# Two heads' states as one block-diagonal operand, diagonal blocks on GpSimd, and a later place for the weights' check

## The chip, the cores and the metric

The kernel runs on one core of a Trainium2 chip. The metric is the time of one execution on the device, in microseconds (us), as the median of several runs.

## The reference, cut to what matters

Three stages follow each other: a linear recurrence per head (four batches, eight heads, 768 steps, head width 48), a gated feed-forward block with a convolution along the sequence, and a sparse attention over four experts. The change touches the first stage alone.

```python
state = np.zeros((B, H, D, D), dtype=np.float32)
for t in range(S):
    kt, vt, rt, wt = (k[:, :, t], v[:, :, t], r[:, :, t], w[:, :, t])
    cur = np.einsum('bhd,bhe->bhde', u[None] * kt, vt)
    y[:, :, t] = np.einsum('bhd,bhde->bhe', rt, state + cur)
    state = wt[:, :, :, None] * state + np.einsum('bhd,bhe->bhde', kt, vt)
...
h = np.maximum(x @ w_in, 0.0)
...
gate = 1.0 / (1.0 + np.exp(-conv_out))
return (h * gate @ w_out).astype(np.float32)
```

## The kernel before, in words

Phase 1 does the recurrence and the feed-forward block together, and then the attention runs by itself. The recurrence is cut into 32 units. A unit is one pair of heads (`hp`, four of them), one half of the sequence (`h`) and one batch; units 0 to 3 are the first half of batch 0, units 4 to 7 its second half, and so on. A unit holds three chunks of 128 steps. Two heads of width 48 lie on the 128 partitions, head j = 0 on partitions 0 to 63 and head j = 1 on 64 to 127.

The program is written as 32 slots and a few more for what is left over; `slot(u)` fixes the order of all instructions on PE, DVE, ACT and POOL by hand. Each of these engines runs its list in that order. In slot u stand the second part of unit u, the first part of unit u + 1 and, from slot 5, two groups of the feed-forward block (`ga` and `ga + 1`, with `ga = 2u - 11`). For a unit the steps are:

- `scan_d`, `scan_f`, `queries` (one slot earlier, DVE, L230 to L245): running products of the decays, and from them K and Q.
- `bonus` (POOL, L250 and L251) and `diag` (DVE, L259), for units from 10 on: the diagonal entry e of each step, one number per head, chunk and step. Units below 10 get e from a product on PE (L302, moved to SBUF by ACT, L304).
- `blocks` (ACT, L266, six instructions a unit): writes e on the diagonal of AT, a 128 x 128 block per head and chunk.
- `scores` (PE, L282) and `masked` (DVE, L288): the entries below the diagonal go into AT.
- `trans`, `state` (PE, L297 and L315): U, the contribution of each chunk to the state. `carry1` (ACT, L322) scales it and moves it from PSUM to `Ss`, with three instructions for a unit with h = 0 and two for one with h = 1. `carry2` (DVE, L329) runs the recurrence over the chunks.
- `yout` (one slot later, PE): L343 multiplies AT with the values; L349 multiplies the state before a chunk with Q, for each head by itself:

```python
for j in range(2 if c else 0):
    p = slice(64 * j, 64 * j + 64)
    nc.tensor.matmul(y[p, cc], Sb[p, c - 1], t["Q"][p, cc], start=False, stop=(cc == CH - 1), ...)
```

- `rows`: Y is moved out of PSUM by ACT (L361), its rest is formed by DVE (L362), and POOL copies four edge columns: before the rest, for h = 1 (L359), or after it, for h = 0 (L365).
- `check` (ACT, L273): bounds on the decays.

In a feed-forward group PE multiplies (L387, nine rows a group), ACT takes the relu and the first tap (L391, L395), DVE adds the other two taps (L406 and L408, or L410 and L411), ACT takes the tanh (L414), DVE multiplies (L424), and PE multiplies again four groups later (L437, six rows). The product hs of L387 has one PSUM buffer.

The raw weights are loaded twice: for the conversion in slots 1 to 9 (`WS`, DVE L82, L83 and L197, POOL L84), and once more for `check_w` (ACT, L208 and L209 over 128 x 768 numbers), which stands in the slots of `WC2`, after the tanh of group ga and the gate and before `carry1`. The load is issued one slot earlier. In a slot with a check the order on ACT is thus tanh of ga, L208, L209, L322, L361, and DVE's L362 needs what L361 writes.

Below, the "mark" of a slot is the start of DVE's L362 in it. The mark of slot u belongs to unit u - 1.

Of the kernel before, what the change touches and what calls it, by code (L numbers as in the profile page):

```python
# [10 lines left out]
F32 = mybir.dt.float32  # L11
# [4 lines left out]
AF = mybir.ActivationFunctionType  # L16
OP = mybir.AluOpType
# [3 lines left out]
B, H, S, D = 4, 8, 768, 48  # L21
DM, FF = 384, 1024
NE, HD = 4, 64
C = 128
NC = S // C
# [4 lines left out]
CH = NC // 2  # L30
# [8 lines left out]
LAG = 4  # L39


X2_ON_DVE, V_ON_DVE, OUT_ON_DVE = (), (1,), (5,)
SCALED_ON_POOL = 13
BONUS_ON_PE = 10


def _f(ap):
# [47 lines left out]
def phase1(tc, nc, a, x2, ident, stat, lim, top, right, left2):  # L95

    s1 = ExitStack()
    cst = s1.enter_context(tc.tile_pool(name="cst", bufs=1, side="left"))
# [12 lines left out]
    T = {}  # L111
    fl = lambda ap: ap.rearrange("p a b -> p (a b)")

    def split(u):
        return u // (2 * HP), u // HP % 2, u % HP

    def load(u):
# [8 lines left out]
        z = ld.tile([128, NRKV], F32, name="rkv")  # L126
        zn = 2 * CH * 64 if u < BONUS_ON_PE else NRKV
        nc.sync.dma_start(z[:, 0:zn], a["rkv"][q, h][:, 0:zn])
# [11 lines left out]
    for j in range(2):  # L140
# [14 lines left out]
                            channel_multiplier=-1)  # L155
    msk = cst.tile([128, CH, C], U32, name="msk")
    nc.vector.tensor_copy(msk, ones3)
    Ss = []
    for i in range(HP):
        t = cst.tile([128, NC - 1, 64], F32, name=f"Ss{i}")  # L160
        nc.gpsimd.memset(t, 0.0)
        Ss.append(t)
    load(1)
# [6 lines left out]
    win = [wt.tile([128, 4, 3, 256], F32R, name=f"win{i}") for i in range(2)]  # L170
    wout = wt.tile([128, NF, DM], F32, name="wout")
    wl = lambda t: t.rearrange("p a b c -> p (a b c)") if len(t.shape) == 4 else t.rearrange("p a b -> p (a b)")

    def load_w(n, i):
        t = RW[n, i] = raw.tile([128, WC], U64 if wide else F32, name="rawt")
        nc.sync.dma_start(t, a[n][i])
# [50 lines left out]
    def scan_d(u):  # L227
        t = T[u]
        t["Dp"] = wk.tile([128, CH, C + 1], F32, name="Dp")
        nc.vector.tensor_tensor_scan(fl(t["Dp"]), t["w"][:, 0:NW], fl(cD), 0.0, op0=OP.mult, op1=OP.add)  # L230
# [16 lines left out]
    def bonus(u):  # L247
        b, h, hp = split(u)
        m = T[u]["rn"]
        nc.gpsimd.tensor_tensor(m, m, T[u]["kn"], op=OP.mult)  # L250
        nc.gpsimd.tensor_tensor(m, m, u_b[:, hp][:, :, None].to_broadcast([128, 2, CH, D]), op=OP.mult)  # L251

    def diag(u):
        t = T[u]
        if u < BONUS_ON_PE:
            nc.vector.tensor_tensor(t["k"], t["k"], t["r"], op=OP.mult)
            return
        e = t["e"] = wk.tile([128, 2, CH], F32, name="e")
        nc.vector.tensor_reduce(e, t["rn"], axis=AX.X, op=OP.add)  # L259

    def blocks(u):
        t = T[u]
        AT = t["AT"] = wk.tile([128, 2, CH, C], F32, name="AT")
        for j in range(2):
            for c in range(CH):
                nc.scalar.activation(AT[:, j, c], ident, AF.Copy, scale=t["e"][:, j, c:c + 1])  # L266

    def check(u):
        t = T[u]
        w, Fp = t["w"], t["Fp"]  # L270
        wc = w[:, 1:].rearrange("p (c t) -> p c t", c=CH)[:, :, 0:C]
        for z in range(2):
            nc.scalar.activation(Fp[:, :, 0:C], wc, AF.Relu, bias=lim[:, z:z + 1], scale=(-1.0, 1.0)[z],  # L273
                                 accum_out=stat[:, 2 * u + z:2 * u + z + 1])
# [15 lines left out]
    def trans(u):  # L290
        b, h, hp = split(u)
        t = T[u]
        n = CH - h
        m = ps_m.tile([128, CH * 128 + 2 * CH], F32, name="m")
        kt = m[:, 0:CH * 128].rearrange("p (c t) -> p c t", c=CH)
        for c in range(n):
            nc.tensor.transpose(kt[:, c], t["K"][:, c], ident)  # L297
        KT = t["KT"] = wk.tile([128, CH, 128], F32, name="KT")
        if u < BONUS_ON_PE:
            es = m[:, CH * 128:].rearrange("p (j c) -> p j c", j=2)  # L300
            for c in range(CH):
                nc.tensor.matmul(es[:, :, c], t["k"][:, c], u_c[:, hp], start=True, stop=True)  # L302
            e = t["e"] = wk.tile([128, 2, CH], F32, name="e")
            nc.scalar.activation(e, es, AF.Copy)  # L304
        nc.scalar.activation(KT[:, 0:n], kt[:, 0:n], AF.Copy)
# [12 lines left out]
    def carry1(u):  # L318
        b, h, hp = split(u)
        t = T[u]  # L320
        for c in range(CH - h):
            nc.scalar.activation(Ss[hp][:, CH * h + c, 0:D], t["U"][:, c], AF.Copy, scale=t["Dp"][:, c, C:C + 1])  # L322

    def carry2(u):
        b, h, hp = split(u)
        Sb = Ss[hp]
        for c in range(CH * h, CH * h + CH - h):
            if c:
                nc.vector.scalar_tensor_tensor(Sb[:, c, 0:D], Sb[:, c - 1, 0:D], T[u]["Dp"][:, c - CH * h, C:C + 1],  # L329
                                               Sb[:, c, 0:D], op0=OP.mult, op1=OP.add)  # L330

    YP = {}

    def yout(u):
        b, h, hp = split(u)
        t = T[u]
        y = ps_m.tile([128, CH, C], F32, name="m")
        Sb = Ss[hp]

        for cc in range(CH):  # L340
            for j in range(2):
                p = slice(64 * j, 64 * j + 64)
                nc.tensor.matmul(y[p, cc], t["v"][:, cc, j], t["AT"][:, j, cc], start=(cc == 0), stop=False,  # L343
                                 skip_group_check=True)
        for cc in range(CH):
            c = CH * h + cc
            for j in range(2 if c else 0):
                p = slice(64 * j, 64 * j + 64)
                nc.tensor.matmul(y[p, cc], Sb[p, c - 1], t["Q"][p, cc], start=False, stop=(cc == CH - 1),  # L349
                                 skip_group_check=True)  # L350
        t["y"] = y

    def rows(u):
# [44 lines left out]
    def conv(g):  # L398
        if not 0 <= g < NG:
            return  # L400
        bh, f = divmod(g, NF)
        h = bh % 2
        (ht, ct), w = G[g], cw[0]
        o, N = 2 * h, HT - 2 + 4 * h
        if h == 0:
            nc.vector.scalar_tensor_tensor(ct[:, 1:N], ht[:, 0:N - 1], w[:, 0, f:f + 1], ct[:, 1:N],  # L406
                                           op0=OP.mult, op1=OP.add)
            nc.vector.scalar_tensor_tensor(ct, ht[:, 1:N + 1], w[:, 2, f:f + 1], ct, op0=OP.mult, op1=OP.add)  # L408
        else:
            nc.vector.scalar_tensor_tensor(ct, ht[:, 1:N + 1], w[:, 0, f:f + 1], ct, op0=OP.mult, op1=OP.add)  # L410
            nc.vector.scalar_tensor_tensor(ct[:, 0:N - 1], ht[:, 3:N + 2], w[:, 2, f:f + 1], ct[:, 0:N - 1],  # L411
                                           op0=OP.mult, op1=OP.add)
        st = ml.tile([128, HT + 2], F32, name="st", bufs=2)[:, 0:N]
        nc.scalar.activation(st, ct, AF.Tanh)  # L414
        G[g] = ht, st
# [13 lines left out]
    def mlp2(g):  # L429
# [9 lines left out]
        if f == NF - 1:  # L439
# [13 lines left out]

    WS = ((1, "win", 0), (2, "win", 1), (3, "win", 2), (4, "wout", 0), (5, "win", 3), (6, "wout", 1), (7, "wout", 2),
          (8, "wout", 3))
    WC2 = tuple((10 + i, ("win", "wout")[i % 2], i // 2) for i in range(8))

    def groups(g, last=False):
        if 0 <= g < NG:
            mlp1(g)  # L460
        if 0 <= g - LAG < NG:
            mlp2(g - LAG)

    def slot(u):

        ga = 2 * u - G0
        s1u, nxt = u < 2 * NU, u + 1 < 2 * NU
        for z, n, m in WS + WC2:
            if u == z - 1:
                load_w(n, m)  # L470
        if s1u:
            trans(u)
        conv(ga - 1)
        if s1u:
            blocks(u)
        if nxt:
            if u + 1 >= BONUS_ON_PE:
                bonus(u + 1)
            scan_d(u + 1)
        for z, n, m in WS:  # L480
            if u == z + 1:
                conv2_w(n, m)
        gate(ga - 1)
        groups(ga)
        if s1u:
            check(u)
        if nxt:
            scan_f(u + 1)
        conv(ga)
        if nxt:  # L490
            queries(u + 1)
        gate(ga)
        for z, n, m in WC2:
            if u == z:
                check_w(n, m)
        if s1u:
            scores(u)
            state(u)
            carry1(u)
        if 0 < u <= 2 * NU:  # L500
            yout(u - 1)
        if nxt:
            diag(u + 1)
        for z, n, m in WS:
            if u == z + 1:
                conv3_w(n, m)
            if u == z:
                conv1_w(n, m)
        if u == 2:
            conv2_cw()  # L510
        if u == 1:
            conv1_cw()
        if s1u:
            masked(u)
        if 0 < u <= 2 * NU:
            rows(u - 1)
        if s1u:
            carry2(u)
        if u == 0:
            load_cw()  # L520
        if u == 18:
            rawc.close()
        groups(ga + 1)
        if u + 3 < 2 * NU:
            load(u + 3)
# [645 lines left out]
```

## Time and profile before

| | |
|---|---|
| median of 3 runs | 640.93 us (636.64, 641.79, 640.93) |
| profiled execution | 636.89 us |
| its span in the trace | 635.2 us |
| busy: PE, DVE, ACT, POOL | 588.3 us (93%), 489.0 us (77%), 419.2 us (66%), 123.6 us (19%) |
| recurrence (L297 to L362) | until 338 us |

The span is the time from the first to the last instruction of the profiled execution; the execution is 1.7 us longer. Busy times are means over stages with different limits, so a stage has to be read by itself: by windows (busy time of each engine in a stretch), by the chain of work that ended last, and by the timeline with the idle time ahead of an instruction and the one that ended it, in square brackets.

### The profile page before, as it was taken

To read this page: it belongs to the slowest core of one execution; us is meant where nothing else is said; L and a number is where in the kernel's file an instruction comes from. 1 tells how busy PE (TensorE), PEld (TensorE's weight loads), DVE (VectorE), ACT (ScalarE), POOL (GpSimd) and SP (SyncE) were. 2 spreads that over 40 slices of the span, in tenths; PEclk is the share of its full clock that TensorE was granted. 3 is DMA by queue.
4 is the path that set the end of the run, shared out by engine and by line. 5 is a ranking of instruction groups with operands and counts; after the bars stand their busy time and mean duration, and the time that the engine had idled before them with its cause. 6 is when DMAs were issued, how large, how long until landed. Compare 5 with 4: busy or idle time off the path is not lost.

```text
span 635.2 us, 11577 instructions
## 1 busy us (share of the span) xinstructions
PE 588.3 (93%) x4038; PEld 468.7 (74%) x4038; DVE 489.0 (77%) x1123; ACT 419.2 (66%) x1101; POOL 123.6 (19%) x158
## 2 busy tenths in 40 slices
PE   5778898899999999999999999899998999899896
PEld 4667776667677777777776786788977887778754
DVE  6999998888889999999965642988747774876561
ACT  4876668788997777777775543765646564656452
POOL 2221221212112133121303600210021002103160
PEclk9768899999999999999999999999998999999998
DMA  8666564757643536445224461553255425322502
GB/s 282 215 219 193 171 190 154 228 162 226 213 158 106 193 111 209 134 128 196 68 76 119 135 177 39 130 150 95 63 138 149 101 88 148 92 74 88 137 3 79
DMA packets 34963, 89.47 MB, mean 141 GB/s; under 512 B 5456, under 2 KB 16208, under 8 KB 34896
## 3 DMA queue, kind: packets, MB, share of 16 engines
q1 hardware_dynamic: 34896, 88.64, 46.6%
q8 instruction: 34, 0.56, 0.4%
q14 instruction: 33, 0.27, 0.1%
HBM read 50.82 MB, written 9.44 MB: 95 GB/s over the span
## 4 chain that ended last, share of the span: by engine, by line
PE 54%; DVE 16%; ACT 15%; DMA 7%; issue 4%; POOL 2%; SPq 2%; DVEq 0%; ACTq 0%; POOLq 0%
PE x L437 11%; PE hs L387 8%; PE m L819 6%; PE st L893 5%; PE m L943 5%; PE t L927 4%; PE m L955 4%; ACT AT L266 4%; PE m L849 3%; DMA x<-x 3%; ACT Fp L273 3%; DVE Ss L329 2%; PE sc L282 2%; ACT st L414 2%; PE m L343 2%
## 5 line engine op out<-in xcount | busy, mean ns | idle before, releaser
L437 PE MATMUL x<-gt,wout 128*128 128x386 f32 (+1 forms) x384 | 133.5, 485 | 0.0
L387 PE MATMUL hs<-X,win 128*128 128x384 f32 (+1 forms) x576 | 119.0, 351 | 6.5 <-ACT ht L391 6.3
L387 PEld LDWEIGHTS hs<-X,win 128*128 128x128 f32 x576 | 99.0, 189 | 15.0 <-ACT ht L391 9.6
L437 PEld LDWEIGHTS x<-gt,wout 128*128 128x128 f32 x384 | 71.9, 189 | 35.1
L907 ACT ACTIVATE A<-sm,mn 128x128 f32<-128x128 f32 (+5 forms) x96 | 63.8, 666 | 27.0 <-DVE mn L906 26.2
L906 DVE CUSTOM_DVE_ANT_0 sm<-st,mask 128x128 f32<-128x128 f32 (+5 forms) x96 | 58.2, 618 | 19.1 <-PE st L893 15.7
L414 ACT ACTIVATE st<-ct 128x382 f32<-128x382 f32 (+1 forms) x64 | 33.5, 523 | 51.5 <-DVE ct L408 26.2
L266 ACT ACTIVATE AT<-ident,e 128x128 f32<-128x128 f32 x192 | 59.2, 388 | 0.0
L927 PE MATMUL t<-ident,A 128*128 128x128 f32 x336 | 53.6, 276 | 1.9 <-ACT T L931 1.0
L424 DVE SCALAR_TENSOR_TENSOR gt<-st,ht 128x382 f32<-128x382 f32 (+1 forms) x64 | 42.6, 666 | 15.7 <-ACT st L414 13.2
L893 PE MATMUL st<-sk,sq 128*128 128x384 f32 (+3 forms) x128 | 44.8, 360 | 2.7 <-DVE mn L906 2.0
L933 DVE COPY T<-t 128x128 f32<-128x128 f32 (+3 forms) x64 | 32.1, 504 | 18.5 <-PE t L927 18.0
L927 PEld LDWEIGHTS t<-ident,A 128*128 128x128 f32 x336 | 40.2, 140 | 8.2 <-issue 2.2
L282 PEld LDWEIGHTS sc<-Q,K 64*128 64x128 f32 x384 | 29.3, 212 | 21.9 <-DVE AT L288 8.6
L931 ACT ACTIVATE T<-t 128x512 f32<-128x512 f32 (+3 forms) x64 | 28.6, 447 | 25.3 <-PE t L927 20.3
L893 PE MATMUL st<-sl,sq 128*128 128x384 f32 (+3 forms) x128 | 41.0, 333 | 4.3 <-DMA sl<-kl 4.3
L943 PE MATMUL m<-T,V 128*64 128x384 f32 (+2 forms) x288 | 43.8, 422 | 0.0
L282 PE MATMUL sc<-Q,K 64*128 64x128 f32 x384 | 36.2, 318 | 7.6 <-DVE AT L288 7.6
L395 ACT ACTIVATE ct<-ht,cwk 128x382 f32<-128x382 f32 (+1 forms) x64 | 39.5, 617 | 2.0
L391 ACT ACTIVATE ht<-hs 128x384 f32<-128x384 f32 (+1 forms) x64 | 31.0, 484 | 13.4 <-PE hs L387 13.4
L273 ACT ACTIVATE Fp<-wkr,lim 128x384 f32<-128x384 f32 x64 | 39.2, 612 | 1.0
L805 POOL TENSOR_TENSOR xs<-x,xs 128x768 fp32r<-128x768 f32 x12 | 22.5, 1889 | 87.7 <-ACT xs L804 84.3
(131 smaller groups left out, 1149.8 us busy)
## 6 DMA issues: line engine op xcount, KB each, us to landing
wkr<-in_wkr SPq DMA_DIRECT2D x31, 578.0 KB, 4.0
rkv<-in_rkv SPq DMA_DIRECT2D x22, 480.0 KB, 3.8
rawt<-in_win SPq DMA_DIRECT2D x8, 768.0 KB, 6.4
rawt<-in_wout SPq DMA_DIRECT2D x8, 768.0 KB, 4.9
sk<-kh SPq DMA_DIRECT2D x32, 192.0 KB, 3.4
sl<-kl SPq DMA_DIRECT2D x32, 192.0 KB, 4.0
x<-x SPq DMA_DIRECT2D x12, 384.0 KB, 3.8
out_dram<-ot SPq DMA_DIRECT2D x24, 192.0 KB, 1.9
```

The source lines that it names most:

```text
L266: nc.scalar.activation(AT[:, j, c], ident, AF.Copy, scale=t["e"][:, j, c:c + 1])
L273: nc.scalar.activation(Fp[:, :, 0:C], wc, AF.Relu, bias=lim[:, z:z + 1], scale=(-1.0, 1.0)[z], accum_out=stat[:, 2 * u + z:2 * u + z + 1])
L282: nc.tensor.matmul(sc[j][:, c], t["K"][p, c], t["Q"][p, c], start=True, stop=True)
L387: nc.tensor.matmul(hs[:, 0:N], win[wi][:, f // 2, i, (f % 2) * 128:(f % 2 + 1) * 128], x[:, i, xi], start=(n == 0), stop=(n == 8))
L414: nc.scalar.activation(st, ct, AF.Tanh)
L424: nc.vector.scalar_tensor_tensor(gt, st, 1.0, ht[:, o:o + N], op0=OP.add, op1=OP.mult)
L437: nc.tensor.matmul(acc[0][i][:, 0:N], wout[:, f, i * 128:(i + 1) * 128], gt, start=(f == 0), stop=(f == NF - 1))
L893: nc.tensor.matmul(st[:, z, 0:n], q[:, qi * C:(qi + 1) * C], k[:, z * n:(z + 1) * n], start=(i == 0), stop=(i == 1))
L906: nc.vector.tensor_tensor_reduce(o3, i3, m3, 1.0, 3e38, op0=OP.add, op1=OP.min, accum_out=mn)
L907: nc.scalar.activation(at, o3, AF.Exp, bias=mn, scale=-1.0, accum_out=rs[:, qi % 3:qi % 3 + 1])
L927: nc.tensor.transpose(pt[:, ki - k0], at[:, ki * C:(ki + 1) * C], self.ident)
L943: nc.tensor.matmul(po[o, lo:HT], V[:, ki, (2 * p + j) * 64:(2 * p + j + 1) * 64], Ts[j][:, ki, lo:], start=(ki == 0), stop=(ki == n - 1))
```

## The change

`Ss` gets room for two blocks a chunk: head 0's state goes to the upper left block, head 1's to the lower right one, and the rest stays at the zeros written at the start. `carry1` becomes two instructions a chunk of 64 partitions each, `carry2` covers 112 columns in place of 48, and `yout` does one product of 128 x 128 a chunk in place of two of 64 x 64. The diagonal blocks of units 0 to 5 stay on ACT; those of units 6 to 31 are written by two instructions on POOL, for units 6 to 9 in the old place, for later ones right behind `diag`, one slot earlier. The weights' check and its loads go from slots 10 to 17 to slots 20 to 27, and the pool of the raw weights is closed after slot 28 in place of 18.

```diff
+DIAG_ON_ACT = 6
...
-        t = cst.tile([128, NC - 1, 64], F32, name=f"Ss{i}")
+        t = cst.tile([128, NC - 1, 2, 64], F32, name=f"Ss{i}")
         nc.gpsimd.memset(t, 0.0)
...
         nc.vector.tensor_reduce(e, t["rn"], axis=AX.X, op=OP.add)
+        blocks(u)
...
         for j in range(2):
-            for c in range(CH):
+            for c in range(CH if u < DIAG_ON_ACT else 0):
                 nc.scalar.activation(AT[:, j, c], ident, AF.Copy, scale=t["e"][:, j, c:c + 1])
+            if u >= DIAG_ON_ACT:
+                nc.gpsimd.affine_select(AT[:, j], t["e"][:, j][:, :, None].to_broadcast([128, CH, C]),
+                                        pattern=[[0, CH], [1, C]], compare_op=OP.is_equal, fill=0.0, base=0,
+                                        channel_multiplier=-1)
...
         for c in range(CH - h):
-            nc.scalar.activation(Ss[hp][:, CH * h + c, 0:D], t["U"][:, c], AF.Copy, scale=t["Dp"][:, c, C:C + 1])
+            for j in range(2):
+                p = slice(64 * j, 64 * j + 64)
+                nc.scalar.activation(Ss[hp][p, CH * h + c, j, 0:D], t["U"][p, c], AF.Copy,
+                                     scale=t["Dp"][p, c, C:C + 1])
...
-        Sb = Ss[hp]
+        Sb = Ss[hp].rearrange("p c j e -> p c (j e)")[:, :, 0:64 + D]
...
-                nc.vector.scalar_tensor_tensor(Sb[:, c, 0:D], Sb[:, c - 1, 0:D], T[u]["Dp"][:, c - CH * h, C:C + 1],
-                                               Sb[:, c, 0:D], op0=OP.mult, op1=OP.add)
+                nc.vector.scalar_tensor_tensor(Sb[:, c], Sb[:, c - 1], T[u]["Dp"][:, c - CH * h, C:C + 1],
+                                               Sb[:, c], op0=OP.mult, op1=OP.add)
...
-            for j in range(2 if c else 0):
-                p = slice(64 * j, 64 * j + 64)
-                nc.tensor.matmul(y[p, cc], Sb[p, c - 1], t["Q"][p, cc], start=False, stop=(cc == CH - 1),
-                                 skip_group_check=True)
+            if c:
+                nc.tensor.matmul(y[:, cc], Sb[:, c - 1].rearrange("p j e -> p (j e)"), t["Q"][:, cc], start=False,
+                                 stop=(cc == CH - 1), skip_group_check=True)
...
-    WC2 = tuple((10 + i, ("win", "wout")[i % 2], i // 2) for i in range(8))
+    WC2 = tuple((20 + i, ("win", "wout")[i % 2], i // 2) for i in range(8))
...
-        if s1u:
+        if u < BONUS_ON_PE:
             blocks(u)
...
-        if u == 18:
+        if u == 28:
             rawc.close()
```

On ACT in slot 12 of the kernel before, from the transposed keys (KT, L305) to the tap of the second group (L395); st is the tanh, AT the diagonal blocks, rawt the check, Ss the state:

```order
L305 ACTIVATE KT<-m 128x256
L414 ACTIVATE st<-ct 128x386
L266 ACTIVATE AT<-ident,e 128x128 x6
L391 ACTIVATE ht<-hs 128x388
L395 ACTIVATE ct<-ht,cwk 128x386
L273 ACTIVATE Fp,stat<-wkr,lim 128x3x128 x2
L414 ACTIVATE st<-ct 128x386
L208 ACTIVATE rawt<-rawt 128x768
L209 ACTIVATE rawt,stat<-rawt,lim 128x768
L322 ACTIVATE Ss_125<-m,Dp 128x48 x2
L361 ACTIVATE Y<-m 128x384
```

On ACT in slot 20 of the changed kernel, the same stretch (line numbers are 3 to 10 higher):

```order
L313 ACTIVATE KT<-m 128x256
L424 ACTIVATE st<-ct 128x386
L401 ACTIVATE ht<-hs 128x388
L405 ACTIVATE ct<-ht,cwk 128x386
L281 ACTIVATE Fp,stat<-wkr,lim 128x3x128 x2
L424 ACTIVATE st<-ct 128x386
L211 ACTIVATE rawt<-rawt 128x768
L212 ACTIVATE rawt,stat<-rawt,lim 128x768
L332 ACTIVATE Ss_125<-m,Dp 64x48 x4
L371 ACTIVATE Y<-m 128x384
```

The six rows of AT are gone, the state takes four rows of 64 partitions in place of two of 128, and the check still stands between the second tanh and the state, in another slot.

On POOL in slots 10 and 11 of the kernel before (rkv is the bonus, YP the edge columns):

```order
L250 TENSOR_TENSOR rkv<-rkv 128x288
L251 TENSOR_TENSOR rkv<-rkv,u_b 128x288
L365 CAST YP<-Y 128x8
L250 TENSOR_TENSOR rkv<-rkv 128x288
L251 TENSOR_TENSOR rkv<-rkv,u_b 128x288
```

On POOL in the same slots of the changed kernel:

```order
L253 TENSOR_TENSOR rkv<-rkv 128x288
L254 TENSOR_TENSOR rkv<-rkv,u_b 128x288
L272 AFFINE_SELECT AT<-e 128x384 x2
L375 CAST YP<-Y 128x8
L253 TENSOR_TENSOR rkv<-rkv 128x288
L254 TENSOR_TENSOR rkv<-rkv,u_b 128x288
```

The two diagonal instructions stand between the bonus, whose sum e they need, and the copy of the edge columns, which now waits behind them.

## Rows read from the trace of the kernel before

**Rows 1.** Windows: busy us (count) PE, PEld, DVE, ACT, POOL; clock; DMA share; GB/s

```profile
100.00:210.00 110.00, 104.47 (x765) 77.34 (x764) 93.14 (x170) 91.09 (x239) 20.10 (x30) 1.00 0.57 179
210.00:290.00 80.00, 79.90 (x606) 61.41 (x607) 76.86 (x139) 61.39 (x171) 20.24 (x24) 1.00 0.48 155
```

**Rows 2.** Chain that ended last, slots 21 and 22: start us, us, what

```profile
226.59 1.75 PE hs L387 x9
...
230.29 0.22 PE m L297 x2
230.51 1.56 PE hs L387 x9
...
235.92 0.80 PE m L349 x12
236.72 1.77 PE hs L387 x9
```

**Rows 3.** Timeline, marks of slots 9, 19 and 27, and PE after the last

```profile
100.15 0.54 DVE L362 TENSOR_TENSOR Y<-m,Y 128x384 fp32r<-128x384 f32 x1
...
210.53 0.55 DVE L362 TENSOR_TENSOR Y<-m,Y 128x384 fp32r<-128x384 f32 x1
...
290.00 0.54 DVE L362 TENSOR_TENSOR Y<-m,Y 128x384 fp32r<-128x384 f32 x1
...
291.43 0.78 PE L387 MATMUL hs<-X,win 128*128 128x388 f32 x3
```

**Rows 4.** Timeline around slot 16: start us, us, engine, line, what [idle before]

```profile
166.17 0.81 POOL L250 TENSOR_TENSOR rkv<-rkv 128x288 f32<-128x288 f32 x1 [8.17 <-DMA rkv<-in_rkv]
...
166.20 1.05 DVE L288 COPY_PREDICATED AT<-msk,sc 128x384 f32<-128x384 uint32 x2
...
168.05 0.56 DVE L362 TENSOR_TENSOR Y<-m,Y 128x384 fp32r<-128x384 f32 x1 [0.80 <-ACT Y L361]
...
168.45 1.84 PE L387 MATMUL hs<-X,win 128*128 128x384 f32 x9 [0.21 <-ACT ht L391]
168.52 0.57 DVE L329 SCALAR_TENSOR_TENSOR Ss<-Ss,Dp 128x48 f32<-128x48 f32 x2
...
170.81 1.84 ACT L266 ACTIVATE AT<-ident,e 128x128 f32<-128x128 f32 x6
...
173.71 0.62 DVE L406 SCALAR_TENSOR_TENSOR ct<-ht,cwk,ct 128x381 f32<-128x381 f32 x1 [0.36 <-ACT ct L395]
...
175.44 0.90 ACT L208 ACTIVATE rawt<-rawt 128x768 f32<-128x768 f32 x1
...
177.37 0.67 ACT L322 ACTIVATE Ss<-m,Dp 128x48 f32<-128x48 f32 x3
...
177.92 0.50 ACT L361 ACTIVATE Y<-m 128x384 fp32r<-128x384 f32 x1
...
178.46 0.56 DVE L362 TENSOR_TENSOR Y<-m,Y 128x384 fp32r<-128x384 f32 x1 [0.99 <-ACT Y L361]
```

**Rows 5.** Timeline after the mark of slot 11

```profile
124.34 1.17 DVE L329 SCALAR_TENSOR_TENSOR Ss<-Ss,Dp 128x48 f32<-128x48 f32 x2
124.48 0.19 POOL L365 CAST YP<-Y 128x8 fp32r<-128x8 f32 x1 [10.16 <-DVE Y L362]
124.63 0.81 POOL L250 TENSOR_TENSOR rkv<-rkv 128x288 f32<-128x288 f32 x1
...
126.07 1.04 DVE L411 SCALAR_TENSOR_TENSOR ct<-ht,cwk,ct 128x385 f32<-128x385 f32 x1
```

**Rows 6.** Timeline at the start

```profile
2.58 1.29 POOL L161 MEMSET Ss<- 128x320 f32 x4
...
3.88 0.52 POOL L154 TENSOR_SCALAR_AFFINE_SELECT Q<-Q 128x384 f32<-128x384 f32 x1
3.98 1.24 DVE L230 TENSOR_TENSOR_SCAN Dp<-wkr,cD 128x387 f32<-128x387 f32 x1 [3.98 <-POOL cD L149]
```

**Rows 7.** Waits of DVE from 57 to 100 us: us in total, times, longest

```profile
DVE ct L406 <- ACT ct L395: 2.2, 4, 1.1
```

## The prediction

> **What bounds the kernel now.** I read the windows first, to split phase 1 into stages, then the chain, then the timeline of a slot in each stage. From 210 to 290 us PE is busy 79.90 of 80 us at the full clock, and DVE 76.86 [rows 1]. The chain there runs through PE alone: from one group's first product to the same place a slot later is 236.72 - 226.59 = 10.13 us [rows 2]. So slots 20 on are bound by PE, with DVE close behind. From 100 to 210 us no engine is full: PE 104.47 of 110, DVE 93.14, ACT 91.09 [rows 1]. The timeline of slot 16 shows why. Mark to mark it takes 178.46 - 168.05 = 10.41 us, and DVE stands still twice: 0.36 us for the tap that ACT writes late because of its six diagonal instructions (1.84 us), and 0.99 us at the mark, for ACT's Y. That Y stands behind tanh, check (177.37 - 175.44 = 1.93 us) and the state's evacuation [rows 4]. This is a ring: DVE's taps, ACT's tanh, check, state and Y, then DVE again. The ten slots 10 to 19 take 210.53 - 100.15 = 110.38 us, the eight slots 20 to 27 take 290.00 - 210.53 = 79.47 us [rows 3].
>
> A second thing lengthens slots. Two DVE instructions for the state take 0.57 us alone [rows 4] but 1.17 us where POOL's bonus product starts right behind the copy of edge columns, and a tap there takes 1.04 us where one alone takes 0.62 [rows 4, 5]: 0.60 + 0.42, about 1.0 us a slot. The masked copy L288 keeps its 1.05 us beside the same POOL product of 0.81 us [rows 4]. The edge copy waits for the mark where the unit of that mark has h = 0, so slots 10 to 13, 18 to 21 and 26 to 29 pay the 1.0 us in full.
>
> **The change part by part.** All sums are made on the profiled execution (span 635.2 us, execution 636.89 us) and then put on the median, 640.93 us, which lies 4.04 us above that execution.
>
> *The product of states.* In a slot with h = 1 twelve rows of 64 x 64 take 0.80 us; after, six rows of 128 x 128. No such row is in the trace. Nearest are the transposes, full array and 128 columns, two in 0.22 us, 0.11 us a row: 0.66 us, 0.14 less. Bounds are 0.80 (no gain) and 0.40 (the old price a row, 0.067 us, for half the rows). And the group behind the product takes 1.77 us, the one behind the transposes 1.56 [rows 2]; I put the 0.21 down to the change of tile shape, which now falls away (bounds 0 and 0.21). PE's slot becomes 10.13 - 0.14 - 0.21 = 9.78 us.
>
> The Trainium skill (TensorEngine Tiling, Tiling Modes, Key Properties) says that tiles of the array work independently and that a change of tiling mode drains the array. By the first half, two 64 x 64 products cost as one whole-array product, so the merge would gain nothing and PE's slot would be 9.92 us; fifteen slots bound by PE would take 0.07 to 0.14 us more, and the median would be 639.2 us, inside the forecast's bounds. By the second half the 0.21 is a drain that goes. The rows agree with the first half only in part: 0.80 us for twelve is 0.133 us a pair, above the 0.11 of a full-array row.
>
> *Diagonal blocks off ACT.* ACT loses 1.84 us a slot in units 6 to 31. On DVE's path this gives back only the 0.36 us. On POOL two instructions come in; the row of the same form is the mask at the start, 0.52 us at 128 x 384 [rows 6]. What it does to DVE beside it no row shows; the bounds are nothing, as L288 beside the bonus, and its whole time, as the state beside the bonus [rows 4, 5]. For units from 10 on the pair starts when e is there, under the two masked copies (1.05 us) and Y, which read PSUM; 2 x 0.52 = 1.04 us fits, and I cost it at nothing. If that cover is too short, DVE loses up to 1.04 us a slot. In slots 6 to 9 the pair comes behind POOL's weight conversion and meets the taps: 0 to 1.04 us a slot, I take 0.52, 2.1 us in all. There DVE waited 2.2 us for ACT's tap in four times [rows 7], which goes.
>
> *carry2, 112 columns.* From two instructions of 48 columns (0.57 us) to a tap of 381 (0.62 each) [rows 4] 64 columns are worth some 0.06 us, 0.13 a slot, on DVE: 0.8 us in slots 0 to 5 and 0.5 in 6 to 9, taken in full. *carry1, twice the instructions.* Three take 177.92 - 177.37 = 0.55 us [rows 4], 0.18 each; halving the partitions should not shorten them (bounds 0.09 and 0.18). ACT has room for it, except in the ring of a check slot: +0.37 (h = 1) or +0.55 us (h = 0). In slot 0, where nothing lies ahead of it, I add 0.5 us.
>
> *Zeroing Ss.* Four writes of 320 numbers take 1.29 us ahead of the first scan, which waits for POOL [rows 6]. Twice the size costs 0 to 1.29 us; I take 0.9.
>
> *The check, moved.* Its loads go with it: eight of 128 x 768 numbers of eight bytes (0.79 MB) over some 80 us add 79 GB/s to the 155 GB/s there; DMA was at 179 with them before [rows 1], and loads are issued a slot ahead, so I cost the DMA at nothing. What is moved is the ring. Slots 10 to 19 lose it: PE needs 9.78 us a slot, DVE (93.14 of 110, and some 0.3 us of gaps and 0.13 of carry2 a slot) about 9.8; I take 9.85, bounds 9.78 and 10.2. Ten slots take 98.5 in place of 110.4: -11.9 us. Slots 20 to 27 get it. From slot 16: 10.41 - 0.36 + 0.13 + 0.55 = 10.73 us for h = 0 without the POOL collision; for h = 1 one evacuation less before (-0.18) and only +0.37, so 10.37. With the collision 1.0 more. Two slots of each kind (20 and 21: 11.37; 22 and 23: 10.37; 24 and 25: 10.73; 26 and 27: 11.73) are 88.4 us in place of 79.5: +8.9 us. Behind the waiting Y on DVE stand the state and the next group's taps, and ACT's next relu comes behind its Y too; PE waits for that one, since hs has one buffer.
>
> *The end of it.* Before, PE was 291.43 - 290.00 = 1.4 us behind the mark at slot 27 [rows 3]; in a ring it follows by 168.45 - 168.05 = 0.4 us [rows 4]. That gives 1.0 us. Slots 28 to 32 are PE's: 5 x 0.35 = 1.75 us. The attention is unchanged.
>
> Sum: start +0.9; slots 0 to 5 +0.8 and +0.5; slots 6 to 9 -2.2 + 0.5 + 2.1 = +0.4; slots 10 to 19 -11.9; slots 20 to 27 +8.9; PE's lag -1.0; slots 28 to 32 -1.75. That is -3.15 us: an execution of 633.7 us where the profiled one took 636.89, and **637.8 us** on the median, 0.5% less.
>
> **The rivals.** *The ring is hidden in slots 20 to 27.* ACT is busy only 61.39 of 80 us there [rows 1], loses the diagonal, and gets 1.93 us of check; if its tanh came early enough, PE would stay the bound at 9.85 us. Then 78.8 in place of 88.4, and no gain by the lag: 637.8 - 9.6 + 1.0 = 629.2 us. For it speaks ACT's share, against it that tanh waits for DVE's taps, whatever ACT has to do, and that slot 16 pays 0.99 us with the same order.
>
> *POOL holds DVE.* The pair on POOL takes longer than the 1.05 us of masked copies and the 0.5 us of Y that cover it, or runs late, and DVE's state and taps collide with it. It decides from about 0.8 us an instruction on. Every slot from 10 on outside the check's would rise to DVE's 9.8 + 1.0 = 10.8 us, 0.95 above my 9.85, in 14 slots: 13.3 us; and slots 6 to 9 pay 2.1 us more. 637.8 + 15.4 = 653.2 us, slower than before. For it speaks the collision of the bonus [rows 5], against it the 0.52 us [rows 6]. The Trainium skill (GPSIMD Engine Reference, Key points) says that POOL shares its SBUF interfaces with VectorE and contends with instructions of two SBUF inputs. By that rule this rival holds wherever the pair slips past the masked copies. The trace agrees in both directions: 0.57 against 1.17 us for the state, no loss for L288.
>
> *All check slots collide.* The bonus of slots 22 to 25 waits for its load; if that lands behind the mark, these four pay 1.0 us as well: 637.8 + 4.0 = 641.8 us, no change.
>
> **How the numbers follow.** About 1%, 6.4 us, is what a measurement of this kernel can tell from no change: its three runs spread by 5 us. Forecast 0.50, all check slots collide 0.21, hidden ring 0.15, POOL holds DVE 0.14. The forecast's own bounds: slots 10 to 19 up to +3.5, check slots by 0.3 us each way (2.4), early slots 2.1 each way (POOL's pair in slots 6 to 9), the product up to +4.2 (15 slots at 10.13 in place of 9.85; a cheaper product gives nothing below DVE's 9.8). Together, not all at one end, that is 633 to 643 us, of which a quarter lies more than 1% below. Faster: 0.15 + 0.12 = 0.27. Slower: the POOL case with a rest of 0.02, 0.16. Within 1%: 0.57. The range runs from 630, near the hidden ring, to 648 us, part of the way to the POOL case.
>
> **What would show it.** In the changed profile, marks 9 to 19 should lie 98 to 100 us apart and marks 19 to 27 about 88; DVE should wait at L372 for ACT's Y by 1.2 to 1.6 us in slots 20 to 27 and nowhere in 10 to 19. PE's rows behind the state product should start without the 0.2 us, and the product take 0.66 us. POOL's pair should end before DVE's state begins. I am wrong if the check slots stay near 10.1 us, if the pair takes over 0.8 us each, or if slots 10 to 19 stay above 10.5 us.

## The result, and the profile after

The changed kernel takes 649.59 us (median of 4 runs, 646.76 to 651.60), the kernel before 639.34 us in the runs beside it: ratio 1.0148, 95% interval 1.0103 to 1.0194. The forecast was 637.8 us, range 630 to 648 us; the result is slower by 1.5%, outside the range and on the other side of no change.

Marks (start of DVE's Y, L372 in the changed kernel) divide the time as in [rows 3]. Timeline of the changed kernel: start us, us, engine, line, what, and in brackets the idle time before it and what ended it.

```profile
102.95 0.56 DVE L372 TENSOR_TENSOR Y<-m,Y 128x384 fp32r<-128x384 f32 x1 [0.36 <-ACT Y L371]
...
204.87 0.56 DVE L372 TENSOR_TENSOR Y<-m,Y 128x384 fp32r<-128x384 f32 x1 [0.35 <-ACT Y L371]
...
299.62 0.56 DVE L372 TENSOR_TENSOR Y<-m,Y 128x384 fp32r<-128x384 f32 x1 [2.30 <-ACT Y L371]
...
345.75 0.56 DVE L372 TENSOR_TENSOR Y<-m,Y 128x384 fp32r<-128x384 f32 x1 [0.58 <-ACT Y L371]
```

| us | before | forecast of the change | after | change |
|---|---|---|---|---|
| to mark 9 | 100.15 | +2.6 | 102.95 | +2.80 |
| slots 10 to 19 | 110.38 | -11.9 | 101.92 | -8.46 |
| slots 20 to 27 | 79.47 | +8.9 | 94.75 | +15.28 |
| slots 28 to 32 | 47.62 | -2.75 (lag, PE) | 46.13 | -1.49 |
| mark 32 | 337.62 | -3.15 | 345.75 | +8.13 |

The profiled executions differ by 13.2 us (636.89 and 650.08), 8.1 of them before mark 32. The other 5 us lie in the attention, which the change doesn't touch: from mark 32 to the end of the span it took 297.6 us in the profiled execution before, 302.7 in the changed kernel's, and 300.0 to 304.9 in the twelve experiments. The kernel before happened to be profiled at the short end. Kernels are therefore compared by their marks below.

The windows that answer to [rows 1] show the two stages change places: PE is nearly full from 100 to 210 us and idle for 8.55 of 80 us from 210 to 290. Columns as there.

```profile
100.00:210.00 110.00, 108.30 (x757) 82.75 (x757) 104.28 (x185) 76.61 (x199) 34.97 (x55) 1.00 0.49 154
210.00:290.00 80.00, 71.45 (x485) 53.14 (x486) 64.44 (x115) 57.28 (x137) 20.06 (x35) 1.00 0.58 188
```

DVE's waits from 210 to 300 us (total us, times, longest) name what ends last there, once a slot:

```profile
DVE Y L372 <- ACT Y L371: 15.8, 8, 2.3
```

The timeline of slot 26 shows what stands ahead of that Y, as [rows 4] did for slot 16:

```profile
282.33 0.53 ACT L424 ACTIVATE st<-ct 128x386 f32<-128x386 f32 x1 [1.30 <-DVE ct L421]
282.76 0.90 ACT L211 ACTIVATE rawt<-rawt 128x768 f32<-128x768 f32 x1
...
283.73 1.05 DVE L296 COPY_PREDICATED AT<-msk,sc 128x384 f32<-128x384 uint32 x2
283.89 0.99 POOL L272 TENSOR_SCALAR_AFFINE_SELECT AT<-e 128x384 f32<-128x384 f32 x2 [6.20 <-DVE e L262]
284.61 0.19 ACT L212 ACTIVATION_READ_ACCUMULATOR rawt<-rawt,lim 128x1 f32 x1
284.70 1.82 ACT L332 ACTIVATE Ss<-m,Dp 64x48 f32<-64x48 f32 x6
286.54 0.49 ACT L371 ACTIVATE Y<-m 128x384 fp32r<-128x384 f32 x1
286.57 0.31 PEld L305 LDWEIGHTS m<-ident,K 128*128 128x128 f32 x3 [2.08 <-ACT Ss L332]
...
287.06 0.56 DVE L372 TENSOR_TENSOR Y<-m,Y 128x384 fp32r<-128x384 f32 x1 [2.28 <-ACT Y L371]
```

The ring is the one forecast (taps, tanh, check, state, Y), but the state's evacuation takes 286.54 - 284.70 = 1.84 us from its start to the start of Y, where three instructions took 0.55 [rows 4] and 1.10 was forecast. Six take 0.30 each, not 0.18, and both DVE and PE stand behind them. POOL's two selects take 0.99 us under the masked copies, which keep their 1.05 us: nobody waits for them.

The chain of the changed kernel in slots bound by PE (start us, us, what) answers to [rows 2]:

```profile
180.30 0.64 PE m L359 x4
180.94 1.60 PE hs L397 x9
...
315.62 0.86 PE m L359 x6
316.48 1.56 PE hs L397 x9
```

The group behind the state product is down from 1.77 to 1.56 us, but the product is up from 0.80 to 0.86.

### The profile page after: what moved, and what is told of

The parts are those of the page before. It is cut to its first block, busy times and chain, and to the rows that moved or that the text cites. A ratio compares the mean times of both kernels' runs of the same rounds, so it can differ in the third digit from the quotient of the medians.

```text
span 648.4 us, 11234 instructions
## 1 busy us (share of the span) xinstructions
PE 591.5 (91%) x3878; PEld 474.2 (73%) x3878; DVE 495.6 (76%) x1123; ACT 405.6 (63%) x1025; POOL 145.4 (22%) x210
## 4 chain that ended last, share of the span: by engine, by line
PE 55%; DVE 16%; ACT 11%; DMA 10%; issue 3%; POOL 2%; SPq 1%; ACTq 0%; DVEq 0%; POOLq 0%
PE x L447 10%; PE hs L397 8%; PE m L829 7%; PE st L903 5%; PE m L953 5%; PE t L937 4%; PE m L965 4%; PE m L859 3%; ACT Ss L332 3%; DMA rkv<-in_rkv 3%; PE sc L290 3%; PE m L354 2%; DVE Ss L340 2%; PE m L359 2%; DMA wkr<-in_wkr 2%
## 5 line engine op out<-in xcount | busy, mean ns | idle before, releaser
L447 PE MATMUL x<-gt,wout 128*128 128x386 f32 (+1 forms) x384 | 133.5, 485 | 0.0
L397 PEld LDWEIGHTS hs<-X,win 128*128 128x128 f32 x576 | 99.5, 190 | 12.9 <-ACT ht L401 11.9
L447 PEld LDWEIGHTS x<-gt,wout 128*128 128x128 f32 x384 | 71.9, 189 | 35.1
L272 POOL TENSOR_SCALAR_AFFINE_SELECT AT<-e 128x384 f32<-128x384 f32 x52 | 25.9, 522 | 132.0 <-DVE e L262 120.6
L903 PE MATMUL st<-sk,sq 128*128 128x384 f32 (+3 forms) x128 | 46.2, 371 | 3.4 <-DVE mn L916 2.6
L434 DVE SCALAR_TENSOR_TENSOR gt<-st,ht 128x382 f32<-128x382 f32 (+1 forms) x64 | 39.5, 617 | 12.0 <-ACT st L424 8.9
L332 ACT ACTIVATE Ss<-m,Dp 64x48 f32<-64x48 f32 x160 | 46.8, 292 | 2.2 <-PE m L323 0.6
```

Source lines behind the costliest of these rows:

```text
L332: nc.scalar.activation(Ss[hp][p, CH * h + c, j, 0:D], t["U"][p, c], AF.Copy, scale=t["Dp"][p, c, C:C + 1])
L397: nc.tensor.matmul(hs[:, 0:N], win[wi][:, f // 2, i, (f % 2) * 128:(f % 2 + 1) * 128], x[:, i, xi], start=(n == 0), stop=(n == 8))
L434: nc.vector.scalar_tensor_tensor(gt, st, 1.0, ht[:, o:o + N], op0=OP.add, op1=OP.mult)
L447: nc.tensor.matmul(acc[0][i][:, 0:N], wout[:, f, i * 128:(i + 1) * 128], gt, start=(f == 0), stop=(f == NF - 1))
L903: nc.tensor.matmul(st[:, z, 0:n], q[:, qi * C:(qi + 1) * C], k[:, z * n:(z + 1) * n], start=(i == 0), stop=(i == 1))
```

## The experiments

The theory (A) was that the doubled evacuations, dear and in the ring of the check, cost the time; the rivals were that POOL's selects hold DVE (B), that the check costs more where PE is the bound (C), and that ACT's time or the loads cost, not the place in the ring (D). The table has the marks of each run's profile; "20 to 27" is the stretch of those slots.

| run | mark 9 | 10 to 19 | 20 to 27 | mark 32 | median us | ratio to before (95%) |
|---|---|---|---|---|---|---|
| states only | 103.48 | 121.82 | 83.76 | 355.39 | 658.30 | 1.0262 (1.0215 to 1.0310) |
| diagonal only | 100.03 | 105.83 | 80.26 | 334.18 | 639.87 | 0.9977 (0.9944 to 1.0011) |
| check only | 100.15 | 101.33 | 89.81 | 337.93 | 641.70 | 1.0008 (0.9978 to 1.0039) |
| grouped | 101.40 | 100.16 | 91.87 | 339.54 | 642.90 | 1.0036 (1.0007 to 1.0065) |
| early check | 102.94 | 102.51 | 82.35 | 333.92 | 636.24 | 0.9921 (0.9893 to 0.9949) |
| diagonal, early check | 99.99 | 99.31 | 81.94 | 328.67 | 633.37 | 0.9876 (0.9835 to 0.9917) |
| grouped, early check | 101.42 | 99.32 | 80.39 | 327.93 | 631.74 | 0.9849 (0.9817 to 0.9881) |
| no block-diagonal | 99.94 | 99.22 | 87.45 | 333.23 | 635.56 | 0.9899 (0.9867 to 0.9930) |
| split | 100.88 | 101.08 | 93.89 | 342.50 | 648.13 | 1.0118 (1.0047 to 1.0189) |
| double | 99.85 | 100.27 | 92.25 | 338.98 | 642.01 | 1.0043 (1.0016 to 1.0069) |
| scratch | 98.87 | 99.87 | 89.55 | 334.94 | 640.23 | 1.0014 (0.9976 to 1.0051) |
| zero on DVE | 99.67 | 99.70 | 80.48 | 326.28 | 630.44 | 0.9880 (0.9842 to 0.9917) |

**One part at a time.** The first three runs are the kernel before with one part of the change each.

*States only* (`Ss`, `carry1`, `carry2` and `yout` of the change's diff; no `blocks` and no `WC2`).

```diff
-        for c in range(CH - h):
-            nc.scalar.activation(Ss[hp][:, CH * h + c, 0:D], t["U"][:, c], AF.Copy, scale=t["Dp"][:, c, C:C + 1])
+            for j in range(2):
...
+                nc.tensor.matmul(y[:, cc], Sb[:, c - 1].rearrange("p j e -> p (j e)"), t["Q"][:, cc], start=False,
```

> The kernel before with the block-diagonal states alone: ACT's diagonal blocks stay, the check stays in slots 10 to 19. Theory A (in the changed kernel the 64-partition evacuations of the states, 0.30 us each, sit in the check's ring): here the ring is in slots 10 to 19, so ten slots pay 0.84 or 1.27 us more each, 10.6 us; with 1.1 us at the start and about 1.3 us of wider carry in slots 0 to 9, less 0.14 us of product in 13 slots, 647 to 651 us against 639, and marks 9 to 19 about 120 us apart instead of 110. Theory B (POOL's selects hold DVE, and the evacuations are not what decides): 639 to 642 us, marks 9 to 19 within 3 us of the kernel before. Both theories: state product 0.86 us for six rows.

Measured: +17.8 us at mark 32 and 658.30 us, more than theory A's 647 to 651; slots 10 to 19 rise by 11.4 us, near its 10.6. Timeline of one turn of the ring:

```profile
114.09 1.82 ACT L324 ACTIVATE Ss<-m,Dp 64x48 f32<-64x48 f32 x6
115.93 0.49 ACT L363 ACTIVATE Y<-m 128x384 fp32r<-128x384 f32 x1
115.96 0.55 PE L297 MATMUL m<-ident,K 128*128 128x128 f32 x3 [2.08 <-ACT Ss L324]
...
116.86 3.28 PE L389 MATMUL hs<-X,win 128*128 128x388 f32 x9 [0.35 <-ACT ht L393]
```

PE is idle for 2.08 us, and the next nine rows take 3.28 us where they take 1.85 later in the trace; the granted clock from 116.8 to 121 us is 0.61, a mean of 2.4 and 1.2 GHz in which the lower one prevails. Two more such stretches follow, behind idle times of 1.52 and 1.17 us ahead of L297, with nine rows in 2.65 and 3.12 us (windows, columns as in [rows 1]):

```profile
144.00:147.20 3.20, 3.20 (x10) 2.58 (x9) 3.17 (x5) 0.87 (x4) 1.67 (x3) 0.50 0.62 173
226.00:229.20 3.20, 3.20 (x10) 2.95 (x10) 3.13 (x5) 1.12 (x4) 1.94 (x3) 0.50 0.70 222
```

A further 4.3 us went in slots 20 to 27, at 10.3 to 10.4 us a slot and 11.27 in the last. From 230 to 300 us the chain runs through ACT and DVE alone; ACT's diagonal blocks, still there, are its largest part (9.2%). How much each part is worth no run takes apart.

*Diagonal only* (`blocks` and `diag` of the diff).

```diff
+            if u >= DIAG_ON_ACT:
+                nc.gpsimd.affine_select(AT[:, j], t["e"][:, j][:, :, None].to_broadcast([128, CH, C]),
```

> The kernel before with the diagonal blocks moved to POOL alone; states, evacuations and check as before. Theory A (evacuations): slots 10 to 19 lose the late tap of 0.36 us, slots 6 to 9 the wait of 2.2 us, so 633 to 637 us, faster than before by about 0.6%, with selects of 0.5 us that nobody waits for. Theory B (POOL holds DVE): slots from 10 on rise by 0.5 to 1 us, 645 to 650 us, with DVE's state or taps lengthened beside the selects.

Measured: -3.4 us at mark 32, with -4.6 in slots 10 to 19 and +0.8 in 20 to 27. The median, 639.87 us, misses theory A's 633 to 637, and its interval holds no change: the gain shows at the marks only, and the attention of this profiled execution is the longest of all, 304.9 us. Theory B falls. In slots 6 to 9 the pair does meet DVE, and the tap that takes 0.61 us alone takes 0.90:

```profile
67.64 0.99 POOL L270 TENSOR_SCALAR_AFFINE_SELECT AT<-e 128x384 f32<-128x384 f32 x2
...
68.13 0.90 DVE L412 SCALAR_TENSOR_TENSOR ct<-ht,cwk,ct 128x381 f32<-128x381 f32 x1
```

Those four slots together moved by only -0.16 us (marks 5 to 9): what the collision costs and what ACT's late tap gave back cancel, as the sum had it (-2.2 + 2.1).

*Check only*, with the pool closed after slot 28.

```diff
-    WC2 = tuple((10 + i, ("win", "wout")[i % 2], i // 2) for i in range(8))
+    WC2 = tuple((20 + i, ("win", "wout")[i % 2], i // 2) for i in range(8))
```

> The kernel before with the check in slots 20 to 27 alone. Theory A: the ring moves with its price of about 1 us a slot, slots 10 to 19 fall by 8 to 9 us and slots 20 to 27 rise by 8 to 9 us: 638 to 642 us. Theory C (the check costs more in slots 20 to 27 than where it was, because PE is the bound there and nothing can be caught up): slots 20 to 27 rise by 13 us or more, 644 to 648 us.

Measured: -9.1 us in slots 10 to 19, +10.3 in 20 to 27 (between theory A's 8 to 9 and theory C's 13, nearer to A), +0.3 at mark 32. The move alone costs nothing that can be measured (ratio 1.0008), and theory C falls.

**The evacuations themselves.** *Grouped*: the changed kernel with the two loops of `carry1` exchanged.

```diff
-        for c in range(CH - h):
-            for j in range(2):
+        for j in range(2):
+            for c in range(CH - h):
```

> The changed kernel with the evacuations in another order: all of one half of the partitions, then all of the other. Theory A1 (switching between partition halves costs 0.12 us each time): instructions of the same half take 0.18 us again, six take about 1.2 instead of 1.82 us, and the run falls by 8 slots of 0.4 to 0.6 us, to 645 or 646 us. Theory A2 (an instruction on 64 partitions takes 0.30 us wherever it stands): 649 to 650 us, no change.

```profile
267.39 1.36 ACT L332 ACTIVATE Ss<-m,Dp 64x48 f32<-64x48 f32 x6
268.77 0.49 ACT L371 ACTIVATE Y<-m 128x384 fp32r<-128x384 f32 x1
```

Six take 1.38 us to the start of Y, not 1.84; -6.2 us at mark 32, of which 2.9 in slots 20 to 27: less there than the 3.2 to 4.8 expected, more in all, since the slots before gain too. It is the alternation of halves that costs: theory A1.

*No block-diagonal*: the changed kernel with `Ss`, `carry1`, `carry2` and `yout` of the kernel before.

```diff
-        t = cst.tile([128, NC - 1, 2, 64], F32, name=f"Ss{i}")
+        t = cst.tile([128, NC - 1, 64], F32, name=f"Ss{i}")
```

> The changed kernel without the block-diagonal states (old states, one evacuation a chunk): diagonal blocks on POOL and the check in slots 20 to 27 as the change has them. Theory A (the evacuations in the ring): slots 10 to 19 about 99 to 101 us, slots 20 to 27 about 89 to 91 us, 639 to 643 us, so that the states alone are worth 6 to 10 us of the changed kernel's loss. If the three parts cost together what they do because of POOL and the check, 646 to 650 us.

Measured: 12.5 us earlier at mark 32 than the changed kernel (7.3 in slots 20 to 27, 2.7 in 10 to 19, 3.0 before, less 0.5 in 28 to 32), better than expected, and 1.0% faster than the kernel before. The states are the part that lost. Three runs built on this one ask what in them.

*Split*: the old compact tile, evacuated by halves in turn.

```diff
-            nc.scalar.activation(Ss[hp][:, CH * h + c, 0:D], t["U"][:, c], AF.Copy, scale=t["Dp"][:, c, C:C + 1])
+            for j in range(2):
+                p = slice(64 * j, 64 * j + 64)
+                nc.scalar.activation(Ss[hp][p, CH * h + c, 0:D], t["U"][p, c], AF.Copy,
+                                     scale=t["Dp"][p, c, C:C + 1])
```

> The run without the block-diagonal states, with one change: each evacuation of a state is two instructions of 64 partitions, in turn one half and the other, into the old compact tile; product and carry as in the kernel before. Theory A (the evacuations are what the states cost): six take 1.82 us, four 1.21, slots 20 to 27 rise from 87.5 to 93 to 96 us, the run from 635.6 to 642 to 646 us. Theory E (the wider carry, the product or the larger state tile cost it): slots 20 to 27 within 2 us of 87.5, the run at 635 to 638 us.

*Double*: each evacuation of all 128 partitions twice, to the same place.

```diff
         for c in range(CH - h):
+            for j in range(2):
```

> The run without the block-diagonal states, with each evacuation of a state done twice, on all 128 partitions, the second one writing the same numbers again. If an instruction on 128 partitions costs 0.18 us in a row (the price of the prediction): six take 1.1 us, slots 20 to 27 rise by 8 times 0.36 or 0.55 us, 3.6 us, to about 91, and the run to 638 to 640 us; the distance to the split run is then the price of switching halves. If six take 1.8 us here too, the number of instructions costs, not the halves: same as the split run.

*Scratch*: the second one of each pair goes to a tile that nobody reads.

```diff
             nc.scalar.activation(Ss[hp][:, CH * h + c, 0:D], t["U"][:, c], AF.Copy, scale=t["Dp"][:, c, C:C + 1])
+            nc.scalar.activation(scr[:, c], t["U"][:, c], AF.Copy, scale=t["Dp"][:, c, C:C + 1])
```

> The run without the block-diagonal states, with each evacuation followed by a second one on 128 partitions that writes the same numbers to a scratch tile nobody reads: as many instructions as in the split run, in the same order of chunks, no two to one address, and no halves. If the number of instructions costs 0.18 us each: four take 0.85, six 1.2 us, slots 20 to 27 rise to about 91 us. If they take 1.2 and 1.8 us as in the split run, then it is two instructions in a row on one chunk that cost 0.30 each, and not the switch of halves.

The six instructions of one slot, in split, then in double, then the first and last two of scratch, which stand apart in the timeline since two lines alternate:

```profile
257.68 1.83 ACT L330 ACTIVATE Ss<-m,Dp 64x48 f32<-64x48 f32 x6
259.53 0.49 ACT L370 ACTIVATE Y<-m 128x384 fp32r<-128x384 f32 x1
```

```profile
255.28 1.66 ACT L329 ACTIVATE Ss<-m,Dp 128x48 f32<-128x48 f32 x6
256.83 0.48 ACT L369 ACTIVATE Y<-m 128x384 fp32r<-128x384 f32 x1
```

```profile
252.88 0.28 ACT L329 ACTIVATE Ss<-m,Dp 128x48 f32<-128x48 f32 x1
253.06 0.29 ACT L330 ACTIVATE scr<-m,Dp 128x48 f32<-128x48 f32 x1
...
253.79 0.33 ACT L330 ACTIVATE scr<-m,Dp 128x48 f32<-128x48 f32 x1
253.97 0.52 ACT L369 ACTIVATE Y<-m 128x384 fp32r<-128x384 f32 x1
```

To the start of Y it is 1.85, 1.55 and 1.09 us, and the medians follow (split lies 2 us above what was expected, with its stretch inside). One instruction is 0.28 us long at either size; the next starts 0.18 us behind it when nothing is in the way (scratch), and only when it has ended when the halves change (split). Slots 20 to 27 go from 87.45 to 93.89 (split), 92.25 and 89.55 us. So split, with the product and carry of the kernel before, gets 6.4 of the 7.3 us that the states cost there. Double fits neither of its expectations: it slows down too, between the two, and since scratch, which differs in the target of the second instruction, does not, that points at writing the same place twice; no run takes that further. Scratch has its start ordered otherwise, its first mark 1.4 us earlier (20.84 against 22.24), so its stretches count and not its sum.

The Trainium skill (ScalarE: Activation LUTs, What ACT_TABLE_LOAD costs) says that activations back to back overlap by about 93 ns; scratch agrees with 0.28 - 0.18 = 0.10 us. For VectorE it has a rule (VectorE: DVE Perf Modes, Two Vector instructions with no wait between them) that an instruction whose operands start in another quadrant of partitions than the last ones is held until all earlier ones have finished. That section has no such rule for ScalarE; split and grouped look like it, a wait at each change of half and none inside one.

**The place in the ring.** *Early check*: the changed kernel with the check ahead of the first gate of the slot, about where ACT had the diagonal blocks.

```diff
         conv(ga - 1)
+        for z, n, m in WC2:
+            if u == z:
+                check_w(n, m)
...
         gate(ga)
-        for z, n, m in WC2:
-            if u == z:
-                check_w(n, m)
```

> The changed kernel with the weights' check put where the diagonal blocks stood on ACT before (ahead of the gate of the group before) instead of behind tanh, in the ring of DVE's taps, tanh, state and Y. Theory A (the ring is what costs; ACT's 1.9 us are free elsewhere): slots 20 to 27 fall from 94.8 to 80 to 84 us and the run to 636 to 640 us. Theory D (the place does not matter, what costs is ACT's time or the loads of these slots): no change, 648 to 651 us.

Measured: slots 20 to 27 take 82.35 us, 12.4 less, and the run is 2% below the changed kernel and 0.8% below the kernel before. The same check, loads and evacuations now leave the stretch 2.9 us above the kernel before, which has no check there: the ring costs, and theory D falls. DVE's waits from 210 to 300 us:

```profile
DVE Y L372 <- ACT Y L371: 1.4, 4, 0.4
```

*Diagonal, early check* is the kernel before with POOL's selects and the check at this place (the diffs of *diagonal only*, *check only* and *early check*); *grouped, early check* adds the block-diagonal states with the loops of *grouped*.

> The kernel before with diagonal blocks on POOL and the check in slots 20 to 27 at the early place; states and evacuations as before. Theory A: slots 10 to 19 about 99 to 101 us, slots 20 to 27 about 80 us, 631 to 636 us, faster than the kernel before by about 1%. If the check's loads or ACT's time cost in slots 20 to 27 wherever it stands, 640 to 644 us.

> The changed kernel with the check at the early place and the evacuations grouped by partition half. If the block-diagonal product is worth its 0.14 us a slot and the evacuations are out of the ring: 630 to 635 us, at or below the run with old states and the early check. If the double evacuations still cost outside the ring: 635 to 640 us.

Both came as expected, but for 81.94 us in place of about 80 in slots 20 to 27 of the first. The first is also *no block-diagonal* with the check alone moved, and that takes 5.5 us off its slots 20 to 27: the ring again. With everything out of the ring the states gain: one slot of PE, from one output product (L443, L447) to the next but one, in the first run and in the second:

```profile
121.56 2.11 PE L443 MATMUL x<-gt,wout 128*128 128x386 f32 x6
...
131.56 2.11 PE L443 MATMUL x<-gt,wout 128*128 128x386 f32 x6
```

```profile
123.54 2.10 PE L447 MATMUL x<-gt,wout 128*128 128x386 f32 x6
...
133.40 2.10 PE L447 MATMUL x<-gt,wout 128*128 128x386 f32 x6
```

10.00 and 9.86 us: 0.14 us a slot. Seventeen slots on, the same product starts at 294.15 and 293.78 us, 172.59 and 170.24 us later, again 0.14 a slot. At mark 32 the second is 0.7 us ahead, though its mark 9 came 1.4 us later; the intervals of the two ratios overlap.

*Zero on DVE*: as the last, with the zeros written by another engine.

```diff
-        nc.gpsimd.memset(t, 0.0)
+        nc.vector.memset(t, 0.0)
```

> The run with grouped evacuations and the early check, with the state tiles zeroed by DVE, idle at the start, instead of POOL. If the zeroing on POOL is what delays the first scan: POOL's 2.36 us leave the chain, the first scan starts at 2.7 to 3.3 instead of 5.05 us and every mark is 1.5 to 2.3 us earlier, 629 to 631 us, which a measurement can hardly tell from 631.7. If the first loads bound the start: first scan at 3.9 us or later, about 1 us.

```profile
1.02 2.61 DVE L164 MEMSET Ss<- 128x640 f32 x4 [1.02 <-PEq L1171]
...
3.55 0.90 DVE L233 TENSOR_TENSOR_SCAN Dp<-wkr,cD 128x387 f32<-128x387 f32 x1
```

The first scan starts at 3.55 in place of 5.05 us, later than the 2.7 to 3.3 expected, held by DVE's own zeroing now, and mark 32 is 1.65 us earlier. At 630.44 us this is the lowest median of all, 1.2% below the kernel before and, by the two ratios, 2.6% below the changed one; by time alone it can't be told from the two runs before it (the ratio of *grouped, early check* is lower still).

## Why the prediction was wrong

At mark 32 the forecast missed by 8.13 + 3.15 = 11.3 us: 6.4 in slots 20 to 27, 3.4 in 10 to 19, 1.3 in 28 to 32 and 0.2 before. The mechanism, a check's ring that moves with the check, was right; a term in it was mis-sized, and that term was taken as free outside it.

*Start, and slots 0 to 9: right.* +2.80 us against +2.6. The zeroing costs 1.06 us (scan at 5.04 in place of 3.98 [rows 6]) against 0.9:

```profile
2.57 2.35 POOL L164 MEMSET Ss<- 128x640 f32 x4
...
5.04 1.24 DVE L233 TENSOR_TENSOR_SCAN Dp<-wkr,cD 128x387 f32<-128x387 f32 x1 [5.04 <-POOL cD L151]
```

*carry1: the step that failed.* "Three take 177.92 - 177.37 = 0.55 us [rows 4], 0.18 each; halving the partitions should not shorten them (bounds 0.09 and 0.18)." The upper bound was taken from instructions that all lie on the same partitions, as if the distance between two starts were a price of the instruction. It is 0.18 only while one may start before the last has ended; in turn by halves it is 0.30. In the ring that is +0.86 (h = 1: four take 1.23 us to the start of Y, two took 0.37) or +1.29 us (h = 0: 1.84 - 0.55), not +0.37 or +0.55: 4 x 0.49 + 4 x 0.74 = 4.9 of the 6.4 us by which slots 20 to 27 missed. A bound from the other side stood in the prediction's own terms: an evacuation that does not overlap at all, 0.67 us for three with starts 0.18 apart, is 0.67 - 2 x 0.18 = 0.31 us [rows 4].

*The check's slots otherwise: a rival that came in part.* Without the states they take 87.45 us, where the prediction's terms less carry1 (88.4 - 3.7) give 84.7. The bonus was to spare slots 22 to 25; in the changed kernel those missed by 0.86, 0.81, 1.58 and 0.57 us, of which carry1's excess is 0.49, 0.49, 0.74 and 0.74. In slot 24 (marks 251.08 to 263.39) the late bonus meets the tap:

```profile
252.29 1.15 POOL L253 TENSOR_TENSOR rkv<-rkv 128x288 f32<-128x288 f32 x1 [2.64 <-DMA rkv<-in_rkv]
...
252.81 1.04 DVE L418 SCALAR_TENSOR_TENSOR ct<-ht,cwk,ct 128x382 f32<-128x382 f32 x1
```

In slots 22 and 23 it meets the state, which takes 1.25 and 1.20 us there and 0.70 in slot 24; in slot 25 the bonus comes ahead of the mark. This is the rival "all check slots collide", in three slots of four and for less than its 1.0 us each. That the ring would not be hidden was right.

*Slots 10 to 19: right but for the same term.* 99.22 us without the states, against 98.5. With them 101.92: Y is late at six marks by up to 0.4 us, 2.1 us in all, since it stands behind the evacuations there too (0.35 us at mark 19, above). "ACT has room for it, except in the ring of a check slot" was wrong, and so was the forecast of no wait there; split, which has the evacuations alone, takes 1.9 of these 2.7 us.

*The product of states: one half right.* Six rows less four are 0.86 - 0.64 = 0.22 us, 0.11 a row of 128 x 128, as estimated from the transposes. But the merge saves nothing on the rows: in the kernel before, the twelve rows of [rows 2] less the eight of a slot with h = 0 are 0.80 - 0.58 = 0.22 us too, 0.11 a pair.

```profile
266.74 0.58 PE m L349 x8
267.32 1.80 PE hs L387 x9
```

The 0.133 us a pair of the prediction had a fixed part in it. Before, 0.80 - 6 x 0.11 = 0.14 us stood with the product and 0.21 behind it; after, 0.64 - 4 x 0.11 = 0.20 stands with it and nothing behind. So the tile shape changed twice before (128 x 64 for AT, 64 x 64, whole array) and changes once now, ahead of the product: the step had it vanish. The waits of PE's weight loads say the same: before, 0.17 us ahead of both L349 and L387, after, ahead of L359 alone. The sum with the group behind is 2.42 in place of 2.57 us, 0.15 a slot (0.14 by the two early-check runs), where 0.35 was forecast. The Trainium skill (TensorEngine Tiling, Key Properties) has a drain at each change of tiling mode; the trace agrees, at 0.14 to 0.21 us each.

*Slots 28 to 32: too large.* -1.49 against -2.75 us. The product gives 5 x 0.15 = 0.75 in place of 1.75, which is most of it. PE follows the mark at slot 27 by 300.03 - 299.62 = 0.4 us, as forecast.

*POOL's selects: right.* 0.52 us each under the masked copies, free from unit 10 on; the rival "POOL holds DVE" had the right side (slower) for a reason that does not occur.

## What to carry to other kernels

Ask of every instruction added not only how long it is but what it can no longer overlap: on ACT, these short instructions cost a full length each where they change between partition halves, so group them by half or keep them on all partitions. And price an addition at the place where it goes: the same check, with the same evacuations, costs 12 us more inside the ring of taps, tanh, check, state and Y than a few instructions earlier on ACT. A change of several parts can hide a good one: two of these three were worth 1.0% together, and the third took it back and more.

## What the runs showed of the hardware

ACT starts an instruction of 48 columns 0.18 us behind the last on the same partitions, 0.30 us behind one on the other half, and 0.26 us (1.55 / 6) where half of them rewrite what the last one wrote. And PE's clock can make a wait dearer than it is: in the run with the states alone gaps of 2.08, 1.52 and 1.17 us on PE were followed by stretches at a granted clock of 0.61, 0.50 and 0.50, in which nine rows took 3.28, 2.65 and 3.12 in place of 1.85 us. The length of a gap does not decide it by itself: one of 1.62 us in the same run (ahead of L297 at 129.95 us) and gaps of up to 1.64 us in the changed kernel brought no such stretch (1.00 from 100 to 345 us). What does decide it, no run shows.
